# One order of steps for another: chunk attention and a multiplicative FFN on one core

## The chip, the core and the metric

The kernel runs on one core of one Trainium2 chip. The metric is the device time of one execution in microseconds (us), as the median of several runs. Engines are called as in the profile: PE (TensorE), DVE (VectorE), ACT (ScalarE), POOL (GpSimd), SP (SyncE). Each works through its own queue in order, and semaphores tie the queues together. DMAs are issued by POOL (the loads) and SP (moves and stores).

## The reference

For each of 8 batches and 8 heads, 576 tokens of width 64 are cut into chunks of 64, and attention stays within a chunk. The result, 4608 tokens of width 512, goes through a feed-forward part without a nonlinearity:

```python
scores = scale * np.matmul(q_c, k_c.transpose(0, 1, 2, 4, 3))
attn = np.exp(scores - max); attn = attn / (sum + 1e-09)
x = np.matmul(attn, v_c)              # then tokens x 512
h = (x @ w1) * (x @ w2) @ w3          # 512 -> 1024 -> 1024
out = h @ w_out                       # -> 512, float32
```

## The kernel before, in words

The work is cut into 18 **pairs** of 256 tokens (4 chunks), p = 0 to 17. The order of all instructions is written out by hand in the string ORDER (lines 9 to 40) as 606 steps; a step is a letter with numbers, and lines 447 and 448 call them one by one. Every instruction is kept behind the one before it on its own engine, so ORDER is the order of each engine's queue. Steps on different engines are tied only by data and buffers.

Steps of a pair, by engine (p is the pair, u a half of it, g = p // 2 a group of two pairs):

- POOL: `q`, `k`, `v` load a pair's queries, keys and values, and `i`, `o`, `h` the weights. `w` and `x` are one-element copies that read a result, so that the loads behind them on POOL wait for it (`x11` reads xn of pair 11).
- DVE: `T` transposes q (s = 0) or k (s = 1) of a pair within blocks of 32 into qkT. `N` takes a reciprocal and scales a half of a pair's attention output into xn. `X` transposes a half of xn, into xt for pairs 0 to 7, into xm from pair 8 on. `M` multiplies the two halves of the hidden layer into ab. `V` transposes w3.
- PE: `S` makes scores: 64 small matmuls for pairs 0 to 7, 32 from pair 8 on. `P` multiplies them with the values (64 or 32 small matmuls, into two PSUM tiles, u = 0 and 1). `A` and `B` are x @ w1 and x @ w2 for one slice j, into the two halves of one PSUM tile: 8 matmuls 256 wide for pairs 0 to 3, which have slices 0 to 3, and 4 matmuls 512 wide from pair 4 on, where slices 0 to 7 stand for two pairs at once (A4.j serves pairs 4 and 5, and so on). `W` folds w3 and w_out into w3o once. `O` makes 256 output tokens: 16 matmuls 512 wide. `D` are idle matmuls at the start.
- ACT: `E` is the exponential of a pair's scores. `C` copies A's half of the PSUM tile to SBUF, where M reads it. `Y` copies an output from PSUM to SBUF, `Z` does so for w3o. `K` converts the first q and k.
- SP: from pair 8 on, `G` moves qkT to qkm and `H` moves xm to xt by DMA between partitions (4 DMAs a step; two steps a group). `Q` stores an output.

Each PE step in code is a loop over `mm` (line 94), so all matmuls carry line 95 in the profile, and all loads line 98 and all moves line 193.

Buffers tie the queues too. **PSUM has four tiles** of two banks (line 88, `bufs=4`), shared by all of S, P (two), A with B, O and W. A tile comes free when E (of S), N (of P), M (of A and B), Y (of O) or Z (of W) has read it. In SBUF there are five qk tiles (free after T), two each of qkT, qkm, xm and e, three xn, four xt, three ab (free after both O of the group), three copies of C, two output tiles (free when stored), and six value buffers, of which pair p takes p % 6 and frees it with its P.

In short, a pair goes q, k, T, (G), S, E, P, N, X, (H), and every two pairs then A, B, C, M for eight slices, and O, Y, Q. The long steps A, B, O and W fill PE while the short ones wait for other engines.

## Time and profile before

| | |
|---|---|
| median of 3 runs | 244.46 us (244.41 to 244.48) |
| span of the profiled execution, first to last instruction | 242.9 us |
| difference of the two | 1.56 us; the profiled execution's own time is not given apart from its span |
| PE, DVE, ACT, POOL busy | 226.7, 154.3, 85.2, 83.7 us |
| matmuls and weight loads | 2753 each |
| first matmul of real work, last matmul's end | 9.8 us, 239.6 us |
| mean granted PE clock | 1.000 |
| issued from POOL and SP, by DMA queue | q0: 18.9 MB, 83.9% of 16 engines' span; q1: 17.8 MB, 24.0% |

A span is counted from the first to the last instruction of the profiled execution. "Busy" on PE is the time in which a matmul is under way; matmuls overlap. In the page's strips the span is cut into 40 slices of 6.07 us, and a digit is the busy share in tenths. In a list of waits the columns are the total in us, how often, and the longest. In an order of time the columns are start, length, engine, line, operation, tiles, count, and in brackets the idle time just before, with what ended it; "issue" stands where the profile shows nothing that was waited for. Because every engine works through ORDER in sequence and no matmul record is missing here, each record can be given to its step, and step times in this text (S7 at 86.63) come from the order of time in that way.

### The profile page before, as it was taken

The numbers are of one execution on the slowest core, as the hardware profiler recorded it, in microseconds if no ns is written. First come the engines' busy times: TensorE is split into PE (matmuls) and PEld (weight loads), VectorE is DVE, ScalarE is ACT, GpSimd is POOL, SyncE is SP. The second block draws the span as 40 slices with busy tenths as digits, with TensorE's granted clock in tenths as the row PEclk, the third lists the DMA queues.
The fourth block names the chain that finished last, engine by engine and source line by source line (L and its number), as shares of the span: only waits on it lengthen the run. The fifth ranks groups of instructions, "written<-read, shape, count | busy, mean of one in ns | idle before, by whom it ended". The sixth has DMA issues, their size and how long they took to land.

```text
span 242.9 us, 6385 instructions
## 1 busy us (share of the span) xinstructions
PE 226.7 (93%) x2753; PEld 120.2 (49%) x2753; DVE 154.3 (64%) x235; ACT 85.2 (35%) x116; POOL 83.7 (34%) x114
## 2 busy tenths in 40 slices
PE   1189989999999999999999999999999999999994
PEld 1147868874445444444444444444444444444443
DVE  1756799699799588999998899918540332143000
ACT  2412423423333344425336234162332332322322
POOL 7856976656986345764160230000000000000000
PEclk9999999999999999999999999999999999999999
DMA  6999999999999999999999793735502200400244
GB/s 173 179 185 181 185 169 200 196 193 171 167 173 218 222 228 259 179 224 196 205 236 223 221 139 91 163 88 209 142 0 89 87 0 0 173 3 1 86 173 173
DMA packets 93597, 37.65 MB, mean 155 GB/s; under 512 B 75008, under 2 KB 86528, under 8 KB 93568
## 3 DMA queue, kind: packets, MB, share of 16 engines
q0 software_dynamic: 82592, 18.88, 83.9%
q1 hardware_dynamic: 9936, 17.83, 24.0%
q10 hardware_dynamic: 1040, 0.52, 0.8%
q8 instruction: 21, 0.34, 0.6%
q14 instruction: 8, 0.07, 0.1%
HBM read 38.80 MB, written 9.44 MB: 199 GB/s over the span
## 4 chain that ended last, share of the span: by engine, by line
PE 72%; DMA 16%; DVE 4%; SPq 3%; POOL 2%; issue 1%; ACT 0%; DVEq 0%; POOLq 0%
PE ab_ps L95 39%; PE o_ps L95 23%; PE w_ps L95 6%; DMA w<-in_moe_w_dram 4%; DMA qkm<-qkT 3%; SPq L193 3%; DMA qk<-in_q_dram 3%; DMA qk<-in_k_dram 3%; DMA xt<-xm 3%; PE pv L95 2%; PE s_ps L95 2%; DVE qkT L201 2%; POOL vbuf L98 1%; POOL w L98 1%; DVE xt L297 1%
## 5 line engine op out<-in xcount | busy, mean ns | idle before, releaser
L95 PE MATMUL ab_ps<-xt,w 128*128 128x512 bf16 (+1 forms) x688 | 127.4, 342 | 0.7 <-DVE xt L297 0.6
L95 PEld LDWEIGHTS <-w 128*128 128x128 bf16 x704 | 67.1, 98 | 56.1 <-issue 1.8
L366 DVE TENSOR_TENSOR ab<-a_sb,ab_ps 128x512 bf16<-128x512 f32 x71 | 47.8, 674 | 43.4 <-ACT a_sb L351 43.1
L351 ACT COPY a_sb<-ab_ps 128x512 f32<-128x512 f32 x71 | 41.6, 586 | 81.3 <-PE ab_ps L95 81.0
L95 PE MATMUL o_ps<-w3o,ab 128*128 128x512 bf16 (+1 forms) x296 | 63.9, 373 | 0.0
L201 DVE STREAM_TRANSPOSE qkT<-qk 128x1024 bf16<-128x1024 bf16 x36 | 45.1, 1291 | 7.2 <-ACT qk L144 5.5
L95 PEld LDWEIGHTS <-ab 128*128 128x128 bf16 x296 | 28.5, 98 | 32.2
L98 POOL DMA_DIRECT2D vbuf<-in_v_dram x40 | 33.9, 855 | 20.4 <-DMA qk<-in_q_dram 5.2
L396 ACT COPY o_sb<-o_ps 128x1024 f32<-128x1024 f32 x17 | 17.2, 1012 | 45.3 <-PE o_ps L95 41.3
L264 DVE TENSOR_TENSOR xn<-pv,rcs 128x512 bf16<-128x512 f32 x36 | 24.9, 692 | 1.4
L98 POOL DMA_DIRECT2D qk<-in_q_dram x23 | 18.1, 790 | 8.9 <-DMA qk<-in_k_dram 2.4
L98 POOL DMA_DIRECT2D qk<-in_k_dram x23 | 18.0, 783 | 6.5 <-DMA vbuf<-in_v_dram 3.7
L234 ACT ACTIVATE e<-s_ps 128x1024 bf16<-128x1024 f32 x16 | 15.9, 1026 | 1.7 <-PE s_ps L95 1.3
L95 PE MATMUL w_ps<-wo,w3T 128*128 128x512 bf16 x64 | 14.0, 379 | 0.0
L305 DVE STREAM_TRANSPOSE xm<-xn 128x512 bf16<-128x512 bf16 x20 | 13.5, 696 | 0.2
L261 DVE RECIPROCAL rcs<-pv 128x8 f32<-128x8 f32 x36 | 6.9, 193 | 10.4 <-PE pv L95 10.4
L98 POOL DMA_DIRECT2D w<-in_moe_w_dram x16 | 11.1, 695 | 5.3 <-DMA wo<-in_moe_w_out_dram 2.9
L95 PEld LDWEIGHTS <-e 64*32 64x32 bf16 (+1 forms) x832 | 7.8, 97 | 8.7 <-issue 6.9
L95 PE MATMUL pv<-vbuf,e 64*32 64x65 bf16 (+1 forms) x832 | 10.2, 197 | 1.8 <-ACT e L234 1.1
L297 DVE STREAM_TRANSPOSE xt<-xn 128x512 bf16<-128x512 bf16 x16 | 11.4, 711 | 0.5
L389 DVE COPY o_sb<-o_ps 128x256 f32<-128x256 f32 x1 | 0.4, 425 | 16.0 <-PE o_ps L95 16.0
L95 PEld LDWEIGHTS <-qkT 32*64 32x64 bf16 x512 | 5.5, 117 | 10.1 <-DVE qkT L201 7.9
(29 smaller groups left out, 54.2 us busy)
## 6 DMA issues: line engine op xcount, KB each, us to landing
out_dram<-o_sb SPq DMA_DIRECT2D x17, 512.0 KB, 3.3
qkm<-qkT SPq DMA_DIRECT2D x40, 128.0 KB, 4.0
vbuf<-in_v_dram POOLq DMA_DIRECT2D x32, 128.0 KB, 8.2
w<-in_moe_w_dram POOLq DMA_DIRECT2D x16, 256.0 KB, 9.9
qk<-in_q_dram POOLq DMA_DIRECT2D x11, 256.0 KB, 6.8
qk<-in_k_dram POOLq DMA_DIRECT2D x11, 256.0 KB, 7.8
xt<-xm SPq DMA_DIRECT2D x40, 64.0 KB, 3.2
wo<-in_moe_w_out_dram POOLq DMA_DIRECT2D x4, 256.0 KB, 7.1
```

The source lines that it names most:

```text
L95: return inorder(nc.tensor.matmul(*a, **kw))
L98: return inorder(nc.gpsimd.dma_start(dst, src))
L193: inorder(nc.sync.dma_start(dst, src))
L201: inorder(nc.vector.transpose(qkT_t[g][:, :, p % 2, s, heads(h)].rearrange("p e h (y t) -> p h t e y", t=2), qk_t[p][:, s, heads(h)].rearr ...
L234: inorder(nc.scalar.activation(e_t[p][:, :, heads(hh)], s_t[p][:].rearrange("p u (h q) -> p u h q", q=CH)[:, :, heads(hh)], Exp, scale=sca ...
L261: inorder(nc.vector.reciprocal(rc, pv[:, :, :, D:W]))
L264: inorder(nc.vector.tensor_mul(xn_t[p][:, u], pv[:, :, :, 0:D], rc.to_broadcast([P, 2, 4, D])))
L297: inorder(nc.vector.transpose(new_xt(g)[:].rearrange("p (o t) -> p o t", o=KO)[:, :, t0:t0 + UT] .rearrange("p o (m y) -> p m o y", y=BL), ...
L305: inorder(nc.vector.transpose(xm_t[g][:, u, :, m].rearrange("p o (c y) -> p c o y", y=BL), xn_t[p][:].rearrange("p u r m d -> p (u r) m d" ...
L351: inorder(nc.scalar.copy(a_t[p, j][:], ps_t[p, j][:, 0, :]))
L366: inorder(nc.vector.tensor_mul(o, view(a_t.pop((p, j))[:]), view(ps_t.pop((p, j))[:, 1, :])))
L396: inorder(nc.scalar.copy(o_sb[:], ps_t.pop(p)[:]))
```

## The change

The 606 steps stay the same, none is added or left out. From the 61st on (behind B0.2) they stand in another order. Steps of one kind still take the pairs in sequence. Two lines of code are added besides: the constant 8 gets the name MOVED, and a value buffer is taken from a list of free ones at v and given back at P, in place of p % 6.

```diff
 B0.2
-C0.2 M0.1 A1.0 T2.0 B1.0 C1.0 M0.2 A1.1 T2.1 q7 k7
-v7 B1.1 C1.1 M1.0 S2 M1.1 A0.3 E2 T3.0 B0.3 C0.3 P2 M0.3 A1.2 N2.0 X2.0 B1.2 C1.2 N2.1 A1.3 X2.1
...
-C3.1 V0 A3.2 M3.1 B3.2 C3.2 V1 A3.3 M3.2 B3.3 C3.3 V2 W0 M3.3 V3 W1 Z0 V4 V5 W2 Z1 V6 V7 T5.0 Z2 W3
-T5.1 q10 k10 T6.0 T6.1 P4 v10 q11 k11 Z3 S5 N4.0 O0 E5 X4.0 N4.1 X4.1 T7.0 O1 T7.1 Y0 Q0 T8.0 P5 v11
-q12 k12 Y1 S6 T8.1 O2 Q1 E6 N5.0 X5.0 N5.1 X5.1 O3 T9.0 T9.1 Y2 G4.0 P6 v12 q13 k13 A4.0 N6.0 B4.0
-G4.1 Y3 X6.0 N6.1 C4.0 A4.1 X6.1 B4.1 C4.1 M4.0 Q2 S7 Q3 M4.1 A4.2 E7 T10.0 B4.2 C4.2 T10.1 P7 v13
-q14 k14 A4.3 M4.2 B4.3 N7.0 C4.3 A4.4 X7.0 M4.3 B4.4 C4.4 N7.1 A4.5 M4.4 B4.5 C4.5 X7.1 S8 M4.5 S9
...
-G8.1 X14.1 A10.7 M10.6 B10.7 N15.0 C10.7 O6 N15.1 M10.7 X15.0 X15.1 H7.0 S16 Y6 S17 O7 E16 E17 H7.1
-P16 Y7 O8 Q6 N16.0 Q7 N16.1 X16.0 X16.1 P17 Y8 A12.0 N17.0 Q8 B12.0 N17.1 C12.0 A12.1 X17.0 B12.1
...
+T2.0 A1.0 B1.0 M0.1 C0.2 A1.1 T2.1 B1.1 M0.2 S2
+C1.0 M1.0 C1.1 A0.3 E2 B0.3 P2 q7 M1.1 C0.3 A1.2 B1.2 M0.3 N2.0 N2.1 A1.3 C1.2 X2.0 X2.1 B1.3 A2.0
+T3.0 C1.3 B2.0 T3.1 S3 C2.0 E3 A2.1 M1.2 v7 M1.3 M2.0 A2.2 P3 B2.1 C2.1 N3.0 N3.1 X3.0 v8 X3.1 B2.2
+T4.0 M2.1 k7 q8 C2.2 A2.3 B2.3 T4.1 C2.3 A3.0 B3.0 M2.2 M2.3 C3.0 A3.1 M3.0 B3.1 S4 C3.1 V0 E4 V1
+A3.2 V2 k8 A3.3 q9 B3.2 M3.1 k9 B3.3 C3.2 W0 V3 Z0 M3.2 W1 V4 V5 V6 C3.3 Z1 W2 Z2 V7 T5.0 W3 M3.3 Z3
+T5.1 P4 S5 T6.0 N4.0 E5 N4.1 T6.1 X4.0 T7.0 T7.1 O0 v9 Y0 q10 X4.1 P5 N5.0 S6 O1 N5.1 E6 X5.0 T8.0
+Y1 P6 S7 X5.1 N6.0 T8.1 T9.0 E7 Q0 Q1 T9.1 q11 O2 k10 A4.0 Y2 N6.1 X6.0 B4.0 C4.0 G4.0 A4.1 M4.0
+C4.1 B4.1 A4.2 P7 C4.2 M4.1 B4.2 O3 X6.1 k11 T10.0 q12 N7.0 X7.0 G4.1 N7.1 A4.3 M4.2 q13 k12 T10.1
+A4.4 Y3 C4.3 B4.3 A4.5 A4.6 B4.4 C4.4 C4.5 q14 T11.0 M4.3 B4.5 S8 T11.1 M4.4 C4.6 S9 k13 X7.1 B4.6
+E8 M4.5 A4.7 B4.7 C4.7 A6.0 M4.6 E9 v10 G5.0 T12.0 G5.1 P8 C6.0 Q2 B6.0 M4.7 A6.1 N8.0 A6.2 T12.1
+N8.1 B6.1 M6.0 C6.1 q15 C6.2 B6.2 P9 M6.1 A6.3 B6.3 M6.2 X8.0 N9.0 v11 A6.4 C6.3 A6.5 N9.1 S10 C6.4
...
+E11 T13.0 B6.7 Q3 N10.1 M6.7 T13.1 O4 P11 X10.0 H4.0 H4.1 Y4 O5 k15 T14.0 A8.0 C8.0 N11.0 G6.0 N11.1
...
+k17 T16.1 B8.5 A8.6 C8.4 C8.5 A8.7 M8.4 x12 v14 B8.6 T17.0 B8.7 A10.0 B10.0 C8.6 M8.5 M8.6 C8.7 v15
+A10.1 M8.7 A10.2 C10.0 G7.1 M10.0 P13 C10.1 B10.1 B10.2 N13.0 C10.2 S14 M10.1 A10.3 N13.1 M10.2
+A10.4 B10.3 B10.4 C10.3 T17.1 E14 X12.0 C10.4 A10.5 M10.3 C10.5 P14 G8.0 M10.4 S15 N14.0 Q5 B10.5
+E15 O6 x11 v16 M10.5 P15 Y6 O7 Y7 N14.1 A10.6 X12.1 X13.0 G8.1 S16 X13.1 N15.0 S17 C10.6 Q6 E16
+B10.6 N15.1 M10.6 A10.7 X14.0 H6.0 E17 B10.7 P16 N16.0 H6.1 C10.7 A12.0 B12.0 A12.1 M10.7 C12.0
...
+B16.7 Q13 O15 M16.6 Y15 M16.7 Q14 O16 Y16 Q15 Q16 O17
...
+MOVED = 8
...
+    vb_t, vb_free = {}, list(vbuf)
...
     def load_v(p):
+        vb_t[p] = vb_free.pop(0)
...
-                load(vbuf[p % 6][at * CH:(at + m) * CH, u, :, 0:D],
+                load(vb_t[p][at * CH:(at + m) * CH, u, :, 0:D],
...
-            if p < 8:
+            if p < MOVED:
...
         e = e_t[p]
+        vb_free.append(vb_t[p])
```

By queue, the parts that the steps below speak of:

- PE before: `W3 P4 S5 O0 O1 P5 S6 O2 O3 P6 A4.0 B4.0 A4.1 B4.1 S7 A4.2`; after: `W3 P4 S5 O0 P5 S6 O1 P6 S7 O2 A4.0 B4.0 A4.1 B4.1 A4.2 P7 B4.2 O3`. PE's queue is the same in both up to `B2.0 S3 A2.1`.
- SP before: `Q0 Q1 G4 Q2 Q3 G5 H4 G6 Q4 H5 Q5 G7 H6 G8 H7 Q6 ...`; after: `Q0 Q1 G4 G5 Q2 Q3 H4 G6 H5 G7.0 Q4 G7.1 G8.0 Q5 G8.1 Q6 H6 H7 ...`.
- POOL before, from q7: `q7 k7 v7 q8 k8 v8 ...` pair by pair to v15, then `x11 q16 k16 v16 x12 q17 k17 v17`; after: `q7 v7 v8 k7 q8 k8 q9 k9 v9 q10 q11 k10 k11 q12 q13 k12 q14 k13 v10 q15 v11 q16 k14 k15 v12 k16 q17 v13 k17 x12 v14 v15 x11 v16 v17`.

More of the change, by code (lines that the diff above doesn't have):

```diff
@@ L11 @@
 v5 S0 T1.0 E0 P0 D0.1.0.4.512 T1.1 q6 k6 v6 N0.0 S1 D1.0.0.5.512 X0.0 N0.1 X0.1 A0.0 E1 B0.0 C0.0 P1
-M0.0 A0.1 N1.0 X1.0 B0.1 C0.1 N1.1 A0.2 X1.1 B0.2 C0.2 M0.1 A1.0 T2.0 B1.0 C1.0 M0.2 A1.1 T2.1 q7 k7
-v7 B1.1 C1.1 M1.0 S2 M1.1 A0.3 E2 T3.0 B0.3 C0.3 P2 M0.3 A1.2 N2.0 X2.0 B1.2 C1.2 N2.1 A1.3 X2.1
-B1.3 C1.3 M1.2 A2.0 T3.1 q8 k8 v8 B2.0 C2.0 M1.3 S3 T4.0 A2.1 E3 M2.0 B2.1 T4.1 q9 k9 C2.1 P3 v9
-M2.1 A2.2 N3.0 B2.2 C2.2 X3.0 A2.3 N3.1 B2.3 X3.1 C2.3 M2.2 S4 M2.3 A3.0 E4 B3.0 C3.0 A3.1 M3.0 B3.1
@@ L21 @@
-E8 A4.6 T11.0 B4.6 E9 T11.1 P8 v14 q15 k15 C4.6 A4.7 M4.6 G5.0 B4.7 C4.7 N8.0 A6.0 M4.7 B6.0 N8.1
-C6.0 G5.1 A6.1 X8.0 B6.1 M6.0 C6.1 X8.1 P9 v15 A6.2 M6.1 N9.0 B6.2 C6.2 N9.1 A6.3 M6.2 B6.3 C6.3
-X9.0 A6.4 M6.3 B6.4 C6.4 X9.1 A6.5 T12.0 H4.0 B6.5 C6.5 M6.4 A6.6 M6.5 B6.6 T12.1 H4.1 C6.6 S10 S11
-M6.6 E10 A6.7 T13.0 B6.7 E11 P10 T13.1 C6.7 O4 M6.7 G6.0 N10.0 N10.1 X10.0 G6.1 P11 Y4 X10.1 O5
-N11.0 N11.1 x11 q16 k16 v16 Q4 X11.0 X11.1 T14.0 A8.0 H5.0 Y5 B8.0 T14.1 C8.0 A8.1 M8.0 B8.1 H5.1
-C8.1 T15.0 A8.2 B8.2 M8.1 C8.2 T15.1 Q5 A8.3 B8.3 C8.3 M8.2 G7.0 S12 M8.3 S13 E12 A8.4 T16.0 B8.4
@@ L27 @@
-E13 G7.1 P12 T16.1 C8.4 A8.5 B8.5 M8.4 C8.5 N12.0 A8.6 M8.5 B8.6 C8.6 N12.1 x12 q17 k17 v17 A8.7
-M8.6 B8.7 C8.7 X12.0 P13 M8.7 A10.0 X12.1 B10.0 C10.0 N13.0 A10.1 M10.0 B10.1 N13.1 C10.1 A10.2
-X13.0 B10.2 M10.1 C10.2 X13.1 S14 S15 M10.2 E14 A10.3 H6.0 T17.0 B10.3 E15 P14 T17.1 C10.3 A10.4
-H6.1 M10.3 B10.4 C10.4 N14.0 A10.5 M10.4 B10.5 G8.0 C10.5 N14.1 A10.6 M10.5 B10.6 C10.6 X14.0 P15
-G8.1 X14.1 A10.7 M10.6 B10.7 N15.0 C10.7 O6 N15.1 M10.7 X15.0 X15.1 H7.0 S16 Y6 S17 O7 E16 E17 H7.1
-P16 Y7 O8 Q6 N16.0 Q7 N16.1 X16.0 X16.1 P17 Y8 A12.0 N17.0 Q8 B12.0 N17.1 C12.0 A12.1 X17.0 B12.1
@@ L33 @@
-M12.0 C12.1 X17.1 A12.2 M12.1 H8.0 B12.2 C12.2 A12.3 M12.2 B12.3 C12.3 H8.1 A12.4 M12.3 B12.4 C12.4
-A12.5 M12.4 B12.5 C12.5 A12.6 M12.5 B12.6 C12.6 A12.7 M12.6 B12.7 C12.7 O9 M12.7 O10 Y9 Q9 A14.0 Y10
-B14.0 C14.0 Q10 A14.1 M14.0 B14.1 C14.1 A14.2 M14.1 B14.2 C14.2 A14.3 M14.2 B14.3 C14.3 A14.4 M14.3
-B14.4 C14.4 A14.5 M14.4 B14.5 C14.5 A14.6 M14.5 B14.6 C14.6 A14.7 M14.6 B14.7 C14.7 O11 M14.7 O12
-Y11 Q11 A16.0 Y12 B16.0 C16.0 Q12 A16.1 M16.0 B16.1 C16.1 A16.2 M16.1 B16.2 C16.2 A16.3 M16.2 B16.3
@@ L38 @@
-C16.3 A16.4 M16.3 B16.4 C16.4 A16.5 M16.4 B16.5 C16.5 A16.6 M16.5 B16.6 C16.6 A16.7 M16.6 B16.7
-C16.7 O13 M16.7 O14 Y13 Q13 O15 Y14 Q14 O16 Y15 Q15 Y16 Q16 O17
+M0.0 A0.1 N1.0 X1.0 B0.1 C0.1 N1.1 A0.2 X1.1 B0.2 T2.0 A1.0 B1.0 M0.1 C0.2 A1.1 T2.1 B1.1 M0.2 S2
+C1.0 M1.0 C1.1 A0.3 E2 B0.3 P2 q7 M1.1 C0.3 A1.2 B1.2 M0.3 N2.0 N2.1 A1.3 C1.2 X2.0 X2.1 B1.3 A2.0
+T3.0 C1.3 B2.0 T3.1 S3 C2.0 E3 A2.1 M1.2 v7 M1.3 M2.0 A2.2 P3 B2.1 C2.1 N3.0 N3.1 X3.0 v8 X3.1 B2.2
+T4.0 M2.1 k7 q8 C2.2 A2.3 B2.3 T4.1 C2.3 A3.0 B3.0 M2.2 M2.3 C3.0 A3.1 M3.0 B3.1 S4 C3.1 V0 E4 V1
@@ new lines @@
+E8 M4.5 A4.7 B4.7 C4.7 A6.0 M4.6 E9 v10 G5.0 T12.0 G5.1 P8 C6.0 Q2 B6.0 M4.7 A6.1 N8.0 A6.2 T12.1
+N8.1 B6.1 M6.0 C6.1 q15 C6.2 B6.2 P9 M6.1 A6.3 B6.3 M6.2 X8.0 N9.0 v11 A6.4 C6.3 A6.5 N9.1 S10 C6.4
+B6.4 X8.1 B6.5 M6.3 C6.5 q16 X9.0 E10 k14 X9.1 M6.4 M6.5 A6.6 B6.6 C6.6 A6.7 C6.7 M6.6 P10 S11 N10.0
+E11 T13.0 B6.7 Q3 N10.1 M6.7 T13.1 O4 P11 X10.0 H4.0 H4.1 Y4 O5 k15 T14.0 A8.0 C8.0 N11.0 G6.0 N11.1
+A8.1 B8.0 T14.1 C8.1 B8.1 X10.1 X11.0 X11.1 A8.2 M8.0 G6.1 Y5 v12 C8.2 A8.3 M8.1 H5.0 T15.0 S12 S13
@@ new lines @@
+H5.1 k16 B8.2 T15.1 C8.3 E12 M8.2 q17 G7.0 E13 B8.3 M8.3 A8.4 Q4 T16.0 B8.4 P12 N12.0 N12.1 v13 A8.5
+k17 T16.1 B8.5 A8.6 C8.4 C8.5 A8.7 M8.4 x12 v14 B8.6 T17.0 B8.7 A10.0 B10.0 C8.6 M8.5 M8.6 C8.7 v15
[3 more added lines that the diff above has]
+B10.6 N15.1 M10.6 A10.7 X14.0 H6.0 E17 B10.7 P16 N16.0 H6.1 C10.7 A12.0 B12.0 A12.1 M10.7 C12.0
@@ new lines @@
+B12.1 M12.0 X14.1 C12.1 A12.2 M12.1 B12.2 N16.1 C12.2 X15.0 v17 A12.3 C12.3 A12.4 B12.3 A12.5 X15.1
+M12.2 M12.3 B12.4 C12.4 X16.0 C12.5 B12.5 A12.6 B12.6 M12.4 C12.6 H7.0 M12.5 M12.6 A12.7 C12.7 B12.7
+P17 H7.1 N17.0 O8 A14.0 B14.0 N17.1 M12.7 Y8 Q7 X16.1 A14.1 X17.0 O9 B14.1 H8.0 A14.2 C14.0 C14.1 Y9
+B14.2 A14.3 X17.1 M14.0 M14.1 C14.2 M14.2 Q8 H8.1 A14.4 A14.5 B14.3 B14.4 Q9 B14.5 A14.6 C14.3 C14.4
+C14.5 B14.6 M14.3 C14.6 A14.7 M14.4 C14.7 M14.5 B14.7 O10 M14.6 A16.0 Y10 B16.0 A16.1 B16.1 O11
@@ L40 @@
+C16.0 Y11 O12 M14.7 Q10 A16.2 M16.0 Y12 A16.3 B16.2 C16.1 Q11 C16.2 A16.4 C16.3 M16.1 B16.3 A16.5
+M16.2 B16.4 O13 Q12 M16.3 C16.4 B16.5 M16.4 A16.6 C16.5 O14 M16.5 Y13 B16.6 Y14 A16.7 C16.6 C16.7
+B16.7 Q13 O15 M16.6 Y15 M16.7 Q14 O16 Y16 Q15 Q16 O17
 """
+MOVED = 8
 LOW, HIGH = 2.0 ** -60, 2.0 ** 60
@@ L246, in do_P @@
             for m in range(4):
-                if p < 8:
+                if p < MOVED:
                     for g in range(NB) if hh is None else (2 * hh, 2 * hh + 1):
@@ L251, in do_P @@
                                lhsT=e[half[r], u, 2 * g + m % 2, m // 2 * BL:(m // 2 + 1) * BL],
-                               rhs=vbuf[p % 6][half[r], u, 2 * g + m % 2, 0:W], start=True, stop=True)
+                               rhs=vb_t[p][half[r], u, 2 * g + m % 2, 0:W], start=True, stop=True)
                 else:
@@ L255, in do_P @@
                         mm(pv[half[g], r, m * W:(m + 1) * W], lhsT=e[half[r], u, 4 * g + m, :],
-                           rhs=vbuf[p % 6][half[r], u, 4 * g + m, 0:W], start=True, stop=True)
+                           rhs=vb_t[p][half[r], u, 4 * g + m, 0:W], start=True, stop=True)
     def do_N(p, u):
@@ L294, in do_X @@
         g, m = divmod(p, 2)
-        if p < 8:
+        if p < MOVED:
             t0 = m * PT + u * UT
@@ L326, in do_AB @@
     def do_AB(p, j, f, which):
-        if p >= 8:
+        if p >= MOVED:
             rhs = new_xt(p // 2)[:].rearrange("p (s o t) -> p o s t", s=2, o=KO)
@@ L359, in do_M @@
             view = lambda t: t.rearrange("p (j t) -> p j t", j=2)
-        elif p < 8:
+        elif p < MOVED:
             o = ab_t[g][:, j]
```

## The prediction

> **What bounds the kernel now.** I read the busy shares first, then the waits of PE, then PE's order of time.

> ```profile
> PE 226.7 (93%) x2753; PEld 120.2 (49%) x2753; DVE 154.3 (64%) x235; ACT 85.2 (35%) x116; POOL 83.7 (34%) x114
> PEclk9999999999999999999999999999999999999999
> DMA  6999999999999999999999793735502200400244
> ```

> PE is busy for 93% at a full granted clock, and the 16 DMA engines are full until about 133 us. The waits of PE say where the rest is:

> ```profile
> PE z_ps L95 <- DVE qkT L201: 7.4, 1, 7.4
> PE z_ps L95 <- DVE zero L114: 1.4, 1, 1.4
> PE pv L95 <- ACT e L234: 1.1, 1, 1.1
> PE z_ps L95 <- issue: 1.1, 1, 1.1
> PE pv L95 <- issue: 0.7, 1, 0.7
> PE ab_ps L95 <- DVE xt L297: 0.6, 2, 0.3
> PE s_ps L95 <- issue: 0.5, 1, 0.5
> ```

> All but the last three lie before 24 us, where the order is not changed. From A1.0 (24.31) to O17 (236.01) PE takes 211.7 us. Laid end to end with the spacings of its own rows (A or B 0.874 in pairs 0 to 3 and 0.864 later, O and W 3.455, S and P 0.645 and 0.63 before pair 8 and 0.285 and 0.38 from it on, 0.10 whenever a full matmul is followed by S or P, and 0.08 after S from pair 8 on) the steps need 209.3. So an order without any wait could win 2.4 us, 1% of the time. It can lose more.

> Two waits are called "issue": PE waited for no other engine. Here they are in the order of time:

> ```profile
> 30.40 0.46 PE L95 MATMUL pv<-vbuf,e 64*32 64x65 bf16 x37
> 31.53 0.30 PE L95 MATMUL pv<-vbuf,e 64*32 64x65 bf16 x27 [0.67 <-issue]
> ...
> 86.63 0.60 PE L95 MATMUL s_ps<-qkT 32*64 32x64 bf16 x51
> 87.72 0.31 PE L95 MATMUL s_ps<-qkT 32*64 32x64 bf16 x13 [0.49 <-issue]
> ```

> Both break a step in the middle. Counted over all records of PE (weight loads, matmuls, waits), the three issue stops end at records 449 (18.51 us), 961 (31.53) and 2753 (87.72): 512 and 1792 apart, which is 2 and 7 times 256. The page has a queue that moves 16 KB pieces,

> ```profile
> q8 instruction: 21, 0.34, 0.6%
> ```

> [...]

> **The change part by part.** The v buffers: values are loaded and used in sequence, so the list gives buffer p % 6 again; nothing. MOVED is 8, as the constant was; nothing. All else is order. No instruction is added or removed.

> **Up to W0: nothing.** P2's stop stays, since PE's list up to it is the same. On DVE, M0.3, N2, X2, T3.0, T3.1 now follow each other from 31.1 us, at 0.65, 0.92, 0.71 and 1.30 less 0.08 overlap each, and T3.1 ends at 37.2; PE comes to S3 at 37.1. But block 1217 begins inside S3, and its piece (35.74) is usable near 38.1. S3 therefore ends near 38.2, as it does now (A2.1 at 38.21). From there to W0 PE does the same work in another order: W0 near 51.95, as now.

> **P4 to S7: 3.2 lost.** Now O0 and O1 stand between S5 and P5, O2 and O3 between S6 and P6. The new order is P4 S5 O0 P5 S6 O1 P6 S7 O2. The block entered at S5 (record 1985) ends after S5 (128), O0 (32) and 96 records of P5: 0.645 + 3.455 + 0.10 + 0.45 = 4.65 us. The next ends after 32 of P5, S6, O1 and 64 of P6: also 4.65. With 6.15 and 6.4 the two stops are 1.5 and 1.7. The shortest interval between two entries anywhere is 4.91, which gives 0.25 each; the slowest piece on the full engines started 5.9 after entry, which gives 3.7 each. I take the rows of the same steps.

> **Stops of now that go: 1.4 gained.** Behind W0 PE now loses 0.6 at S7, 0.28 between S10 and S11 (G5's last landing, 112.89), 0.17 at A10.0, 0.17 at A12.1, and one change from full to small matmuls less is 0.10.

> **PSUM: 1.85 lost.** There are four tiles. The new order sets several A before their B and S beside A, so that all four are in use; then the next step waits until M has read its tile. From a B's start: 1.07 to C's start, 0.585, 0.04, 0.67, 0.04 to PE, together 2.4 (B4.3 at 91.29, M4.3's end 93.66). Until that need PE does:
> - B4.4 B4.5 S8, then S9: 2 x 0.864 + 0.10 + 0.285 = 2.1; wait 0.3.
> - B4.7 A6.0 and half of P8: 2.0; wait 0.4.
> - B6.1 B6.2 P9, then A6.3: 2.2; wait 0.2. B6.6 A6.7 P10, then S11: 0.2.
> - B10.4 A10.5 P14, then S15: 2.2, but E14 (1.02) stands before C10.4 on ACT, so M10.4 ends 2.95 after B10.4's start: 0.75.

> The trace has no wait of this kind; each may be 0 (if the releases come sooner) or about 0.3 more, so 0 to 3.3 in all. I take the sums.

> **Loads.** k7 goes behind v7 and v8: 1.7 us each later, landing near 69.8; T7.1 ends at 71.2, and S7 is at 74.9 even without stops. Later q and k go ahead of v; v10 (for P10) passes nine loads, and is issued near 99, 13 us ahead of its use. On POOL x12 now holds up v14, v15, x11, v16: N12.1 ends near 133, v14 lands about 5 us later, P14 is at 147. N14.0 waits for x11 (three xn buffers), ready near 137 against 148. Without that cover each us late is a us of PE.

> **Moves on SP: 0, with thin cover.** From the last transpose to the last landing the rows give G4 11.8, G5 13.4, H4 10.8, G6 8.0, H5 about 11. The new order leaves 14.1, 15.3, 12.0, 9.1 and 12.1. Q2 and Q3 go behind G5, which helps it. Q6 now stands before H6 and waits for Y6: O6's start + 4.7, Q6 0.4, eight issues 4.4 to the last, 2 to 2.5 to land, 11.5 to 12, and A12.0 comes 12.04 after O6 plus waits. I count 0; it may be 1.

> **O's as tail.** O8 to O14 are spread among A14 and A16. M14.0 must wait for O9 and M16.0 for O11 (three ab buffers), near 184.5 and 206; the PSUM tiles wanted next, at 187 and 209, come free by then. The last steps O15, O16, O17 and their copies and stores have the distances of now. Nothing.

> **Sum.** +3.2 - 1.4 + 1.85 = +3.65. PE's last matmul moves from 239.64 to 243.3, the span from 242.9 to 246.5. The runs' median 244.46 is 1.56 above the span of the profiled execution; I leave that as it is: **248.1 us**, 1.5% slower.

> **Rivals.**
> 1. Not slower: the block supply doesn't limit, the stops at P2 and S7 being accidents of their places. For it: only three of some 20 entries show a stop. Against it: the multiples of 256, and the pieces before each. It decides at 4.65 us from entry to the usable block. P5 and P6 then run through (-3.2), P2's 0.67 goes and S3 waits for T3.1 instead (0.9 with X2.1): -0.4 against now at W0. 244.46 - 0.4 - 1.4 + 1.85 = 244.5. With PSUM waits shorter than my sums it is faster, down to 242.7 with none.
> 2. Transfers come late: loads that x11 and x12 now hold back run beside G6, H4, H5, each with about 1 us of cover, and Q6 holds H6. Some 3 more: 251. For it: landings of 6 to 9 us where the engines are full. Against it: the extra waits of PE give the moves time.
> 3. PSUM tiles are bound to the release that stands last in the order of steps, not to the one that comes first in time. Then A2.1 waits for E3 (1.2), O7 for Y6 (0.8), A10.6 for Y7 (1.25), O12 for Y11 (1.25), by 4.7 from an O's start to its Y's end (O9 to Y9) against 3.46 of O: 4.5 more, 252.6.

> **How the numbers follow.** The forecast has 0.66, rival 1 0.15 (0.05 of it faster, 0.07 the same), rival 2 0.12, rival 3 0.05; 0.02 is left for an order whose waits nearly all vanish (0.01 faster, 0.01 same). About 0.2% (0.5 us) is what a measurement of this kernel can tell from no change. Small block waits (0.5 in place of 3.2) with PSUM as summed give 245.4; block waits of 2.5 each and rival 2 in part give 251.3. Some of the forecast's low side falls within 0.2%: 0.03. Faster 0.06, same 0.11, slower 0.83; range 245.2 to 251.3.

> **What will show it.** Right: issue stops of 1 to 2 us inside P5 and P6, at records 256 apart; no stop at S7; W0 near 52; waits of PE for DVE ab at S9, A6.3, S11 and S15 of 0.2 to 0.8; last matmul near 243. Wrong: P5 and P6 unbroken (rival 1), waits for DMA at S12, A8.0, A10.0 or A12.0 (rival 2), or for ACT after O6, O7 and O11 (rival 3).

## The result, and the profile after

| | before | after |
|---|---|---|
| median, us | 244.44 (244.24 to 244.48, 4 runs) | 255.75 (255.62 to 258.34, 4 runs) |
| span of the profiled execution, us | 242.9 | 253.4 |
| A1.0 starts, W0 starts, us | 24.31, 51.95 | 24.05, 51.27 |
| PE's last matmul ends, us | 239.64 | 250.16 |

The change makes the kernel slower: after over before is 1.049 by the means of the runs, with an interval of 1.0445 to 1.0535 (1.046 by the medians). The forecast was 248.1 with a range to 251.3, so the direction was right and the size was not. The line numbers of the new kernel are 1 higher at `mm` (L96), 5 at M (L371) and C (L356).

The page of the new kernel, busy shares and strips:

```profile
PE 229.3 (90%) x2753; PEld 120.4 (48%) x2753; DVE 153.0 (60%) x235; ACT 83.8 (33%) x116; POOL 83.6 (33%) x114
PEclk9999999999999999999999999999999999999999
DMA  7999999999999999999574997420504302220424
```

PE does the same 2753 matmuls at a full clock, and its share falls from 93% to 90%: PE stands still more. The waits of PE in the new kernel (what waited, for what, us in total, times, longest):

```profile
PE ab_ps L96 <- ACT a_sb L356: 6.8, 9, 1.2
PE pv L96 <- issue: 1.9, 2, 1.7
...
PE s_ps L96 <- DVE ab L371: 0.9, 2, 0.7
PE s_ps L96 <- DVE qkT L205: 0.5, 1, 0.5
PE ab_ps L96 <- DMA xt<-xm: 0.4, 1, 0.4
...
PE pv L96 <- DVE ab L371: 0.3, 1, 0.3
```

The last five were forecast in kind: stops inside P, S waiting for M's release of a PSUM tile, S3 waiting for T3.1, A12.0 for H6, and P8 for M's release of a tile. The first line is the largest, and nothing in the prediction speaks of it: PE waits for ACT's C. Before, this pair does not occur in the list.

Idle time in this list is shorter by some 0.17 us than what a wait costs (for B4.1 0.67 and 0.84), because a full matmul's record is 0.38 us long where the next one starts 0.216 after it (0.864 for the four of a slice). So I counted as the prediction did, from start to start, against the spacings of PE's own rows. From A1.0 to O17 the excess is 2.4 us before and 13.15 after. In the new kernel, the places above 0.06, by cause:

| cause | steps | us |
|---|---|---|
| B starts only when its own C has ended | B4.1 B4.2 B4.3 B4.5 B6.0 B6.2 B10.6 B12.5 B12.7 B14.7 B16.3 B16.7 | 9.03 |
| blocks of 256 PE instructions | P5 0.32, P6 1.70, P2 0.13 | 2.15 |
| S waits for a PSUM tile | S11 0.22, S15 0.77 | 0.99 |
| transposes and moves | S3 0.52, A2.0 0.10, A12.0 0.43 | 1.05 |

At B6.0, P8's wait for a tile (0.3 in the list) lies under the 0.90 that is put down to C.

The block stops, in PE's order of time in the new kernel (start, length, engine, line, operation, count, idle time before):

```profile
70.00 0.58 PE L96 MATMUL pv<-vbuf,e 64*32 64x65 bf16 x51
70.77 0.24 PE L96 MATMUL pv<-vbuf,e 64*32 64x65 bf16 x13 [0.20 <-issue]
...
75.14 0.43 PE L96 MATMUL pv<-vbuf,e 64*32 64x65 bf16 x34
77.23 0.31 PE L96 MATMUL pv<-vbuf,e 64*32 64x65 bf16 x30 [1.66 <-issue]
```

P5 breaks after 51 matmuls and P6 after 34. The two stops end at records 2242 and 2498, 256 apart, and the 16 KB pieces at 68.35 and 74.78 start 2.4 us before each end (2.3 to 2.6 in the kernel before). S7 is now whole.

The new kind of wait, first on PE (the end of B4.0 and A4.1, then B4.1 and A4.2):

```profile
82.68 1.68 PE L96 MATMUL ab_ps<-xt,w 128*128 128x512 bf16 x7
85.02 1.89 PE L96 MATMUL ab_ps<-xt,w 128*128 128x512 bf16 x8 [0.67 <-ACT a_sb L356]
```

and on ACT in the same stretch (C4.0, C4.1):

```profile
83.52 0.58 ACT L356 COPY a_sb<-ab_ps 128x512 f32<-128x512 f32 x1 [0.67 <-PE ab_ps L96]
84.39 0.58 ACT L356 COPY a_sb<-ab_ps 128x512 f32<-128x512 f32 x1 [0.28 <-PE ab_ps L96]
```

C4.1 ends at 84.39 + 0.58 = 84.97, and B4.1 starts 0.05 later, though B4.1 reads nothing of C4.1: C4.1 reads A's half of the tile, B4.1 writes the other half. The new order has `A4.1 M4.0 C4.1 B4.1`: C stands **ahead of the B of its own slice**. In ORDER before, C stands behind its B at every slice. In the new one 22 C's stand ahead (C4.1 C4.2 C4.3 C4.5 C4.6, C6.0 C6.2 C6.4 C6.7, C8.0 to C8.3, C10.1 C10.5 C10.6, C12.3 C12.5 C12.7, C14.7, C16.3 C16.7). For each of the 22, B starts after C's end, and for 12 of them PE loses time by it.

The trace of the kernel before shows the same tie from the other side. C reads A's half alone, but in all 72 slices it starts only when B has ended, within 0.06 us. For C12.2 on ACT:

```profile
172.32 0.59 ACT L351 COPY a_sb<-ab_ps 128x512 f32<-128x512 f32 x1 [1.14 <-PE ab_ps L95]
```

A12.2 had ended at 171.42, B12.2 ended at 172.28.

The price depends on what PE has to do between A and B. With nothing, A's last matmul ends 1.03 after A's start, and C takes 0.58, with a step of 0.04 and one of 0.05 on either side: B starts 1.70 after A where 0.86 would do, 0.84 lost (B4.1, B12.7, B14.7, B16.7). Where C must also wait on ACT behind another C, it is 1.3. ACT around B12.5 in the new kernel (the two copies C12.4 and C12.5 in one line), and PE there:

```profile
178.94 1.07 ACT L356 COPY a_sb<-ab_ps 128x512 f32<-128x512 f32 x2 [2.87 <-PE ab_ps L96]
```

```profile
175.71 3.19 PE L96 MATMUL ab_ps<-xt,w 128*128 128x512 bf16 x14
180.06 3.61 PE L96 MATMUL ab_ps<-xt,w 128*128 128x512 bf16 x16 [1.16 <-ACT a_sb L356]
```

C12.4 waits for B12.4 (its end 178.90), C12.5 goes behind it and ends at 180.01, and B12.5 starts at 180.06.

### The profile page after: what moved, and what is told of

It reads as the page before. It is cut to its first block, busy times and chain, and to the rows that moved or that the text cites. A ratio compares the mean times of both kernels' runs of the same rounds, so it can differ in the third digit from the quotient of the medians.

```text
span 253.4 us, 6402 instructions
## 1 busy us (share of the span) xinstructions
PE 229.3 (90%) x2753; PEld 120.4 (48%) x2753; DVE 153.0 (60%) x235; ACT 83.8 (33%) x116; POOL 83.6 (33%) x114
## 4 chain that ended last, share of the span: by engine, by line
PE 80%; DVE 6%; ACT 5%; issue 3%; DMA 3%; SPq 2%; DVEq 0%
PE ab_ps L96 43%; PE o_ps L96 23%; PE w_ps L96 5%; ACT a_sb L356 4%; PE z_ps L96 3%; PE s_ps L96 3%; PE pv L96 2%; DMA raw<-in_q_dram 2%; DVE qkT L205 2%; SPq L197 2%; DVE xn L269 2%; DVE ab L371 1%; DVE xt L302 1%; DMA xt<-xm 1%; ACT e L238 1%
## 5 line engine op out<-in xcount | busy, mean ns | idle before, releaser
L96 PE MATMUL ab_ps<-xt,w 128*128 128x512 bf16 (+1 forms) x688 | 129.5, 342 | 7.7 <-ACT a_sb L356 6.8
L96 PEld LDWEIGHTS <-w 128*128 128x128 bf16 x704 | 67.3, 98 | 63.7 <-issue 9.8
L371 DVE TENSOR_TENSOR ab<-a_sb,ab_ps 128x512 bf16<-128x512 f32 x71 | 47.7, 678 | 67.2 <-ACT a_sb L356 36.8
L356 ACT COPY a_sb<-ab_ps 128x512 f32<-128x512 f32 x71 | 41.0, 587 | 85.9 <-PE ab_ps L96 85.9
L96 PE MATMUL o_ps<-w3o,ab 128*128 128x512 bf16 (+1 forms) x296 | 64.7, 374 | 0.0
L205 DVE STREAM_TRANSPOSE qkT<-qk 128x1024 bf16<-128x1024 bf16 x36 | 45.7, 1291 | 5.5 <-ACT qk L145 5.3
L96 PEld LDWEIGHTS <-ab 128*128 128x128 bf16 x296 | 28.4, 98 | 32.3
L96 PE MATMUL w_ps<-wo,w3T 128*128 128x512 bf16 x64 | 14.0, 380 | 0.0
L96 PE MATMUL pv<-vbuf,e 64*32 64x65 bf16 (+1 forms) x832 | 10.5, 198 | 3.3 <-issue 1.9
L96 PEld LDWEIGHTS <-e 64*32 64x32 bf16 (+1 forms) x832 | 7.9, 97 | 10.5 <-issue 7.9
L412 DVE STREAM_TRANSPOSE w3T<-w 128x1024 bf16<-128x1024 bf16 x8 | 9.3, 1216 | 1.7 <-DMA w<-in_moe_w_dram 1.7
## 6 DMA issues: line engine op xcount, KB each, us to landing
w<-in_moe_w_dram POOLq DMA_DIRECT2D x16, 256.0 KB, 9.8
qk<-in_q_dram POOLq DMA_DIRECT2D x11, 256.0 KB, 10.6
qk<-in_k_dram POOLq DMA_DIRECT2D x11, 256.0 KB, 10.6
wo<-in_moe_w_out_dram POOLq DMA_DIRECT2D x4, 256.0 KB, 7.1
```

The costliest lines, as they stand in the source:

```text
L96: return inorder(nc.tensor.matmul(*a, **kw))
L205: inorder(nc.vector.transpose(qkT_t[g][:, :, p % 2, s, heads(h)].rearrange("p e h (y t) -> p h t e y", t=2), qk_t[p][:, s, heads(h)].rearr ...
L356: inorder(nc.scalar.copy(a_t[p, j][:], ps_t[p, j][:, 0, :]))
L371: inorder(nc.vector.tensor_mul(o, view(a_t.pop((p, j))[:]), view(ps_t.pop((p, j))[:, 1, :])))
L412: inorder(nc.vector.transpose(w3T_t[f][:].rearrange("p k (f y) -> p f k y", y=BL), w3[:, NB * f:NB * (f + 1), :].rearrange("p f (k x) -> p ...
```

## The experiments

The theory after the result: **a C ahead of its B makes B wait for C** and costs 9.0 us; the rest is blocks, tiles and one move. The rival readings: PE and ACT get in each other's way on one PSUM tile, or PE is late for another reason, and C's end stands before B's start by accident. Runs made together share runs of the kernel before; their medians were 244.57 (e1 to e4), 244.68 (e5 to e8) and 244.77 us (e9 to e11). The traces of e5 to e11 lack 22 of PE's 2753 matmul records each, so step times from them are good to some 0.2 us.

### e2: the suspected cost alone, put into the kernel before

C12.0 to C12.7 go ahead of their B; nothing else.

```diff
-... Y8 A12.0 N17.0 Q8 B12.0 N17.1 C12.0 A12.1 X17.0 B12.1 M12.0 C12.1 X17.1 A12.2 M12.1 H8.0 B12.2 C12.2 ...
+... Y8 A12.0 N17.0 Q8 C12.0 B12.0 N17.1 A12.1 X17.0 C12.1 B12.1 M12.0 X17.1 A12.2 M12.1 H8.0 C12.2 B12.2 ...
```

> The kernel before, with the eight copies C12.0 to C12.7 put right ahead of their B instead of behind it. Theory 1: each B12.j starts 1.70 us after its A (1.03 for A, 0.04, 0.59 for C, 0.04) in place of 0.86, so eight times 0.84 = 6.7 us more: 251.1. Rival (PE stops in the changed kernel for want of PSUM tiles): M frees its tile no later than now, so nothing, 244.4, or a little faster, as C is done sooner.

Measured: 251.62 us (250.93 to 252.12), ratio 1.0285 (1.0251 to 1.032). PE in a stretch of pair 12; each line is B12.j with the next A:

```profile
171.58 1.89 PE L95 MATMUL ab_ps<-xt,w 128*128 128x512 bf16 x8 [0.67 <-ACT a_sb L351]
174.14 1.89 PE L95 MATMUL ab_ps<-xt,w 128*128 128x512 bf16 x8 [0.67 <-ACT a_sb L351]
```

In the kernel before, the same matmuls run without a break:

```profile
171.69 8.58 PE L95 MATMUL ab_ps<-xt,w 128*128 128x512 bf16 x39
```

Now a slice takes 2.56 us in place of 1.73. Seven B's lose 0.84 each, and B12.0 loses 1.41, as C12.0 waits behind Y8: 7.3 in all, measured 7.05. Eight exchanged steps on ACT's queue cost 2.9% of the kernel.

### e9: the same order, but B writes a tile of its own

For pair 12, B takes another PSUM tile than A.

```diff
-                mm(ps_t[p, j][:, which, i * n:(i + 1) * n],
+                mm((ps_t, pb_t)[which][p, j][:, which, i * n:(i + 1) * n],
...
+        pb_t[p, j] = psum("b_ps") if p == 12 else ps_t[p, j]
```

> The kernel before with C12.0 to C12.7 ahead of their B, as in the kernel that took 251.6 us, but B12.0 to B12.7 write a PSUM tile of their own in place of the second half of A's tile. Theory 1a (B waits for C because both use one tile, and the wait is kept per tile, not per half): the eight stops of 0.84 go, and four tiles are enough for A12.j, B12.j and the next pair: 244.5 us, between 244 and 245.3. Rival 1b (PE can't write PSUM at full pace while ACT reads it, or C ahead costs by its place on ACT): the stops stay, 250 or more.

Measured: 245.64 us (244.9 to 245.99), ratio 1.0031 (1.0016 to 1.0047). PE in the same stretch:

```profile
171.72 1.03 PE L95 MATMUL ab_ps<-xt,w 128*128 128x512 bf16 x4
172.58 1.03 PE L95 MATMUL b_ps<-xt,w 128*128 128x512 bf16 x4
173.45 1.03 PE L95 MATMUL ab_ps<-xt,w 128*128 128x512 bf16 x4
```

The steps follow each other by 0.86 again, with C still ahead of B. So PE keeps its 0.86 here while ACT reads another tile, and C's place does no harm by itself. In this program the wait is kept **for the whole tile**: in the new kernel's 22 slices and the eight of e2, B stands behind C and starts after C's end though it writes the other half, and in the 72 slices of the kernel before, C stands behind B and starts after B's end though it reads the other half. The written order decides which waits for which. What is left above the kernel before, 0.9 us (244 to 245.3 was expected), has its place: B12.0's own tile is one that O8 used, and B12.0 waits 1.2 us for Y8 to read it.

### e1: the new kernel with each C right behind its B

```diff
-C4.1 B4.1 A4.2 P7 C4.2 M4.1 B4.2 ... A4.4 Y3 C4.3 B4.3
+B4.1 C4.1 A4.2 P7 M4.1 B4.2 C4.2 ... A4.4 Y3 B4.3 C4.3
...
-C16.6 C16.7 B16.7
+C16.6 B16.7 C16.7
```

> The changed order, but each of the 22 copies C that stand ahead of their own B are put right behind it; all else stays. Theory 1 (B may not write its half of a PSUM tile until a C that stands ahead of it has read the other half; the changed kernel loses 9.0 us of PE at 12 such B's): those stops vanish. Some of the tile waits that the prediction summed come back (S9 0.3, P8 0.4, A6.3 0.2), since PE is no longer late there. 255.7 - 9.0 + 0.9 = 247.6 us, between 246.5 and 249. Rival (PE stops there because all four PSUM tiles are in use and ACT is late; where C stands doesn't matter): above 253.

Measured: 250.7 us (250.17 to 252.84), ratio 1.0268 (1.0221 to 1.0316). That is above the 246.5 to 249 expected. All twelve stops are gone, but only 5 of the 9 us come back. PE's waits in e1:

```profile
PE pv L96 <- issue: 2.4, 3, 1.6
...
PE s_ps L96 <- DVE ab L371: 1.0, 3, 0.7
PE ab_ps L96 <- DVE ab L371: 0.8, 3, 0.5
```

No line for a_sb is left, and waits for M's release of a tile (DVE ab) are more. Start to start the excess is 8.5: 2.0 for P5 and P6, 0.65 at P2, and 2.05 for the tile waits at S9, P8, A6.3, S11 and S15, three of which were covered in the new kernel because PE came late there anyway. Another 1.36 are tile waits at A8.4, A8.5, A8.6 and A10.3: C8.2 and others now come later, and with them M and the release. A12.0 loses 0.59. The last 1.6 us are of a kind that I hadn't expected. The windows of e1 around the stop in P6 (window, us, then per engine busy time and count for PE, PEld, DVE, ACT and POOL, then granted PE clock, DMA share, GB/s):

```profile
76.00:78.00 2.00, 0.56 (x67) 0.52 (x69) 1.97 (x4) 0.49 (x1) 0.49 (x1) 1.00 1.58 260
78.00:80.00 2.00, 2.00 (x52) 0.92 (x41) 2.00 (x3) 1.02 (x1) 0.81 (x2) 0.55 1.91 177
80.00:82.00 2.00, 2.00 (x7) 0.77 (x6) 1.97 (x4) 0.00 (x0) 1.03 (x2) 0.59 1.42 287
```

After the 1.64 us stop (77.44) the granted clock is about half for 3 us, and O2 takes 1.58 longer. The two runs with a mean clock of 1.000 took 250.17 and 250.51, so the kernel's time hangs on this by less than 1.58; what takes the place of the dip in them was not profiled.

### e3 and e4: shift the block limits in the kernel before

PE's first step makes 12 or 40 more idle matmuls (their results are read by nobody), and every later block limit falls 24 or 80 records earlier in the work.

```diff
-R0 R1 v0 q1 k1 i0 v1 i1 i2 q2 k2 v2 i3 q3 k3 v3 q4 k4 v4 o h0 h1 D0.0.0.16.64 K0 T0.0 K1 T0.1 q5 k5
+R0 R1 v0 q1 k1 i0 v1 i1 i2 q2 k2 v2 i3 q3 k3 v3 q4 k4 v4 o h0 h1 D0.0.0.28.64 K0 T0.0 K1 T0.1 q5 k5
```

(e4: `D0.0.0.56.64`.)

> The kernel before, with 12 more idle matmuls (24 records of PE) in its first step, where PE has nothing to do until 9.8 us. Theory 2 (PE's instructions come in blocks of 256, usable some 5.0 to 5.3 us after PE enters the block ahead): all later block limits move 24 records forward in the order. The one in P2 falls early in P2 and leaves a stop of 0 to 0.15, the one in S7 falls where no stop is left: 0.8 to 1.4 us faster, 243.1 to 243.7. Rival (the stops in P2 and S7 are accidents of those steps): no change, 244.4, the stops in the same matmuls as now.

> The kernel before, with 40 more idle matmuls (80 records of PE) in its first step, again within the time in which PE waits for the first transposes. Theory 2: the limits move 80 records forward and fall so that two of them are crossed quickly three times: stops near 40 us (2.4), 75 us (3.0) and 90 us (1.7) in place of 1.2 in all, at records 193 more than a multiple of 256: some 5 us slower, 248 to 250. Rival (accidents of P2 and S7, or the idle matmuls' own time): 244.4 to 244.6.

e3: 245.66 us (244.52 to 246.9, 12 runs), ratio 1.0043 (1.0022 to 1.0063). Expected was a gain, so the time was a miss. The mechanism is seen: S7's stop moves from its 51st matmul to its 39th and halves (0.49 to 0.25 idle), and the one in P2 is gone. But the gain isn't kept: in this profile A1.0 comes 0.33 later, A2.0 waits 0.71 for X2.1 in place of 0.45, and 0.29, 0.28 and 0.64 appear at S4, P6 and S17. That these follow from the stops that went is not shown: A2.0's wait is 0.5 to 1.1 in e2, e7, e9, e10 and e11 too, where the order up to there is that of before.

e4: 254.09 us (253.69 to 254.54), ratio 1.0391 (1.0358 to 1.0424), slower as expected and by more. PE around S6 in e4:

```profile
79.64 0.67 PE L95 MATMUL s_ps<-qkT 32*64 32x64 bf16 x59
84.01 0.23 PE L95 MATMUL s_ps<-qkT 32*64 32x64 bf16 x5 [3.70 <-issue]
```

This stop of 3.70 us, and another of 2.50 in P3 (43.96), end at records 2497 and 1474, within one record of 4 times 256 apart, and the pieces at 81.60 and 41.77 start 2.4 and 2.2 us before their ends. After each the granted clock is half (0.50 from 86 to 88 us and from 44 to 46), which costs another 1.7 and 1.4 us. A1.0 comes 1.4 later: behind a stop of 1.0 us, now inside S1, the five idle matmuls take 2.31 us in place of 1.25. The 40 matmuls themselves cost nothing, since the wait for the first transposes shrinks by as much (5.18 us in place of 7.36) and S0 starts at 9.78, as before (9.82). Forty idle matmuls in the first microseconds cost 9.5 us, by the places at which PE's instruction blocks begin and by the slow stretches behind the stops. That the supply of blocks can set the end is shown with this: at the stops of these runs, the next block was usable 4.3 to 7.1 us after PE's entry into the one before.

### e5: e1 with the old PE order from O1 to A4.2

```diff
-O0 P5 S6 O1 P6 S7 O2 A4.0 B4.0 A4.1 B4.1 A4.2 P7 B4.2 O3
+O0 O1 P5 S6 O2 O3 P6 A4.0 B4.0 A4.1 B4.1 S7 A4.2 P7 B4.2
```

(PE's part; Y and E move with it on ACT.)

> The changed order with each C behind its B (250.7 us), and PE's 14 steps from O1 to B4.2 put back as they were in the kernel before (O0 O1 P5 S6 O2 O3 P6 A4.0 B4.0 A4.1 B4.1 S7 A4.2), with their Y and E on ACT. Theory 2 (blocks of 256 of PE's instructions; stops of 0.33 in P5 and 1.68 in P6 in the kernel it starts from): these two go, and a stop of about 0.5 in S7 is back: 1.5 less, 249.2, between 248.4 and 249.7. Rival (P6 stops for want of something in that stretch that the place of O doesn't change, such as e or values): no change, 250.2 to 251.

Measured: 253.6 us (253.33 to 253.98), ratio 1.0358 (1.0315 to 1.0401). A miss: 2.9 us slower than e1, not faster. The stops in P5 and P6 are gone, S7's is back (0.5), and A4.0 starts at 82.61 (83.44 in e1, with the half clock ahead of it), but P6 now comes at 81.97 in place of 75.37. N6 needs P6 and stands ahead of T8.1 and T9 on DVE's queue in the new order, so the transposes (from 83.32, in e1 from 77.15), G4 behind them and the scores of pairs 8 and 9 come late. PE in e5 there:

```profile
98.06 0.21 PE L96 MATMUL s_ps<-qkm 64*64 64x64 bf16 x1 [0.49 <-DMA qkm<-qkT]
100.39 1.12 PE L96 MATMUL s_ps<-qkm 64*64 64x64 bf16 x63 [2.12 <-DMA qkm<-qkT]
```

and then the clock is half again (0.50 from 102 to 104 us). So the new order of O and P isn't free to be undone: DVE's order is built on it. What the two block stops cost by themselves is not measured by this run.

### e6 and e8: S and P later where they waited for a tile

e6 is e1 with S8 and S9 behind B4.6, P8 behind B6.0, S15 behind B10.5, and Q6 behind H6.1. e8 is e5 with the same moves.

```diff
-B4.5 C4.5 S8 T11.1 M4.4 S9 k13 X7.1 B4.6 ... P8 Q2 B6.0 ... S15 N14.0 Q5 B10.5
+B4.5 C4.5 T11.1 M4.4 k13 X7.1 B4.6 S8 S9 ... Q2 B6.0 P8 ... N14.0 Q5 B10.5 S15
```

> The changed order with each C behind its B (250.7 us), and four places mended: S8 and S9 behind B4.6, P8 behind B6.0, S15 behind B10.5 (each gives M one more slice of time to free its PSUM tile), and Q6 behind H6.1. Theory 3 (waits for a PSUM tile, as summed in the prediction, and the store in front of H6): S9 0.32, P8 0.53, S15 0.76 and A12.0 0.59 go: 2.2 less, 248.5, between 248 and 249.2. Rival (what is spared is lost again at the next tile, since M is late for it too): above 249.8.

> The changed order with each C behind its B, and the edits of both other kernels of this kind: PE's steps from O1 to B4.2 back as before, and the four places mended. If the terms simply add: 250.7 - 1.5 - 2.2 = 247.0, 1.0% above the kernel before; what is left is A8.4 with A8.6 and A10.3 (1.3), A6.3 and S11 (0.4) and S3. Rival (the terms cover each other): 248 or more.

e6: 250.04 us (248.66 to 251.92), ratio 1.0227 (1.0164 to 1.0291). The waits at S9, P8 and S15 are gone (1.6 in e1), and A12.0's falls from 0.59 to 0.15. About 1.0 us comes back as waits of 0.29 to 0.35 at A4.7, A6.2 and O6. The interval overlaps that of e1, so the two medians decide nothing between them. e8: 252.26 us (249.88 to 252.74), ratio 1.0279 (1.0217 to 1.034), with a single wait of 1.8 us at S9 for G4 and the half clock behind it. Both took longer than expected (248.5 and 247.0). Each undone edit moves the loss, or part of it, to a neighbour.

### e7, e10 and e11: can S7's stop be won in the kernel before?

In e10, S7 and E7 go behind B4.2, P7 behind B4.3, and Q2, Q3 behind G5. e11 is the move of Q2 and Q3 alone. e7 is e10 with one load in a wrong place: v13, which overwrites the value buffer of pair 7, stands ahead of P7, so pair 7 is computed with pair 13's values.

```diff
-M4.0 Q2 S7 Q3 M4.1 A4.2 E7 T10.0 B4.2 C4.2 T10.1 P7 v13 q14 k14 A4.3 M4.2 B4.3
+M4.0 M4.1 A4.2 T10.0 B4.2 S7 C4.2 E7 T10.1 A4.3 M4.2 B4.3 P7 v13 q14 k14
```

> The kernel before, with S7 (and E7) behind A4.2 and B4.2, P7 behind B4.3, and the stores Q2 and Q3 behind G5. Theory 2 says that S7's stop (0.58) goes, since PE enters that block 1.7 us later; Q2 and Q3 no longer run beside G5, so S11's wait for G5 (0.28) may go too: 243.6 to 243.9. Rival (what is won is given back at the next wait that is as yet hidden, as with the 12 idle matmuls): 244.4 or more.

> The kernel before, with S7 (and E7) behind B4.2, P7 behind B4.3 and the loads v13, q14, k14 still behind P7, and the stores Q2 and Q3 behind G5. Theory 2: S7's stop for a block of instructions (0.58) goes, as PE enters the block 1.7 us later, and G5's last landing no longer holds S11 (0.28): 0.86 less, 243.6 to 243.9. Rival (what is won is given back at the next hidden wait): 244.4 or more.

> The kernel before, with the stores Q2 and Q3 behind G5 on SP and nothing else. Theory: G5's landing, which holds S11 for 0.28, comes sooner by what the two stores took of the DMA engines: 0.2 to 0.3 less, 244.2 to 244.4. Rival: G5 is issued when T11 is done and Q2 and Q3 have landed by then (their landings are at 95.8 and 97.5, G5's first issue at 99.5), so nothing, or the stores now delay G5's own landings and H4: 244.5 to 245.

e7: 257.91 us, ratio 1.0544 (1.0507 to 1.0581). P7 has to wait 12.4 us for v13's transfer; the run says nothing on S7. e10: 244.75 us (244.45 to 245.65, 12 runs), ratio 1.000 (0.9986 to 1.0015); expected was a gain of 0.86. S7 is whole, and the time is given back right behind it. PE in e10 (A4.4 behind P7):

```profile
92.69 2.53 PE L95 MATMUL ab_ps<-xt,w 128*128 128x512 bf16 x10 [0.71 <-DVE ab L366]
```

P7 now holds two of the four tiles, and A4.4 has to wait for the one that M4.2 reads; M4.2 stands behind T10.0 and T10.1 on DVE (89.59 to 92.08) and ends at 92.64. e11: 244.46 us (244.19 to 245.2, 12 runs), ratio 0.9988 (0.9974 to 1.0002). S11's wait for G5 (0.28) is gone in its profile, and the median is 0.3 lower, as expected; but the interval takes in no change, so this measurement can't tell.

## Why the prediction was wrong, point by point

**Up to W0: 0 forecast, 0.7 gained.** P2's stop should have stayed; in the new kernel's profile it is 0.13 in place of 0.73, because its piece started 2.1 us after PE entered the block before, not 2.5. S3's block, which the prediction had at 38.1, was there before PE came to it at 37.34. In e1, with the same PE order up to there, P2's stop is 0.65. So this term moves by half a us from one execution to the next. Over all profiles W0 starts at 51.3 to 52.0 with the new order up to there, and at 51.8 to 52.4 with the old one. S3 waits 0.52 for T3.1, which the prediction named under its first rival.

**P4 to S7: 3.2 forecast, 2.0 measured.** Place and kind were right: stops inside P5 and P6, at records 256 apart, none at S7. The intervals between block entries were right as well (4.65 forecast; 4.62 and 4.76 without the stops). The size of one failed: the block behind S5's entry was usable after 4.94 us, where 6.15 was taken from the kernel before. For P6 6.46 was measured and 6.4 forecast. The reading that a block is asked for about when PE enters the one before goes by the starts of the 16 KB pieces alone (their distances are in the last section). Rival 1 is out.

**Stops of now that go: 1.4.** Right: S7, S10 to S11, A10.0 and A12.1 show none. The five numbers there add to 1.32; S7's stop costs 0.68 from start to start, not 0.6, which makes it 1.4.

**PSUM: 1.85 forecast.** Right in mechanism and size, but covered in part. In e1, without the waits for C, the five places show 0.32, 0.53, 0.22, 0.22 and 0.76, together 2.05, where 0.3, 0.4, 0.2, 0.2 and 0.75 were summed. In the new kernel itself only S11 and S15 lose by it (0.99): PE reaches S9 and A6.3 late, and P8's wait lies under that of B6.0 for C6.0.

**Loads and O's tail: 0.** Right: no wait of PE for a load or for Y shows between A1.0 and O17.

**Moves on SP: 0, or 1 for Q6 ahead of H6.** A12.0 waits 0.43 for H6. Rival 2 would have needed 3.

**The step that failed** is "All else is order": it put the place of C against B at nothing, without a reason. The PSUM sums even start C 1.07 us after B's start, that is, behind B everywhere, and the new order has it ahead at 22 slices. Rival 3 asked whether waits are bound to the written order, but for the release of a tile to another step, where they are not (A2.1, O7, A10.6 and O12, the places that it named, follow without a wait). Within one tile they are: at all 22 slices with C ahead, B starts 0.05 us or more after C's end. The term is +9.03, by e2 0.84 for each exchanged pair, and by e9 nothing when the two halves are two tiles.

The sum, made again with what was measured: 3.65 forecast; blocks -1.2, tiles -0.85, A12.0 +0.4, before W0 -0.7, C ahead of B +9.0. That gives +10.3, against 10.5 between the two spans. (The medians are 11.3 apart; the profiled execution has the shortest span of the four, 253.4 against 254.1, 254.3 and 256.0.) Without C ahead of B the same sum leaves +1.3, so the forecast had the direction for a sound reason, but most of the loss has another cause. The prediction could have found it: the front of this text says that A and B go into two halves of one tile and that C reads A's, the diff shows `A4.1 M4.0 C4.1 B4.1`, and in the trace before each C waits for B's half, which it doesn't read.

What stays open: what the block stops cost by themselves in the new order (e5 changed DVE's waits with it), and the exact worth of the half clock in e1. No run has ACT reading one half of a tile while PE writes the other, since the wait keeps them apart. No version here is faster than the kernel before by more than the measurement can tell.

## What to carry to other kernels

When the order of a queue written by hand is changed, list for each buffer the reads and writes in the new order, and look for a write that has come behind a read which it does not need; its price was the read's whole way there and back (0.84 us each time with nothing else between), and a tile of its own took it away (e9). An order is a set of covers: of the edits here that took stops away, e1 gave back nearly half of them at other places, e6 about half by its profile, and e3, e5, e8 and e10 kept nothing of it in their times, so price the place behind a stop before you price the stop. Where an engine stops for no reason in the profile, count its records and look for equal distances (256 here).

## What was not expected of the hardware

**The granted clock after a stop.** In these runs 3.41 us at half clock follow stops of 1.6 us (e1, e6), 1.8 (e8), 2.12 (e5), 2.50 and 3.70 (e4), and cost 1.4 to 1.7 us where it was counted (e1, e4, e6). In e7 the half clock lasts through the rest of the 12.4 us stop and 3.8 us more. But the new kernel's stop in P6 of 1.66 us, at the same place as e1's, is followed by 1.00.

The traces show more. Counted from a trace's first record of a full clock, every change of the granted clock in all 13 traces falls on a whole multiple of 3.41 us (in the kernel before the full clock is recorded for 228.69 us, 67 times 3.413, in the new one for 235.52, 69 times), and not on the stops themselves: in e1 the stop ends at 77.44 and the half clock begins at 78.21. In e1 the stretch of 3.41 us with the stop and the next one, and in the new kernel the one with the stop (columns as above):

```profile
74.80:78.21 3.41, 1.77 (x129) 1.15 (x129) 3.38 (x5) 1.01 (x1) 1.20 (x2) 1.00 1.71 247
78.21:81.62 3.41, 3.41 (x33) 1.31 (x20) 3.38 (x6) 1.02 (x1) 1.64 (x3) 0.50 1.68 222
```

```profile
75.60:79.01 3.41, 1.78 (x99) 1.23 (x100) 3.38 (x6) 1.34 (x2) 0.30 (x1) 1.00 1.70 232
```

PE is busy alike in both stretches with the stop (1.77 and 1.78), but with O's full matmuls (128 rows and columns of PE) for 0.64 us in e1 and 0.88 in the new kernel. Before PE's last matmul the clock falls seven times in these traces, and the stretch ahead of each fall has full matmuls for 0.15 to 0.85 us; apart from the stretches inside e7's long stop, which stay at half, the new kernel's is the only other one there under 1.2. The time of all matmuls doesn't tell them apart: e6's stretch ahead of its fall was busy for 1.85 us, small matmuls of S and P included, more than the new kernel's 1.78. So two stops of the same length at the same place, 1.64 and 1.66 us, came with half clock in one execution and without it in the other, and what was found to differ is where the stretches lie and how long full matmuls ran in them. No run was made to test whether that decides it. One of the new kernel's four runs (258.34 us) has a mean clock of 0.993, as the profiled runs of e1 and e6 with their one half stretch have.

**Blocks of instructions.** From PE's entry into a block to the usable next one it took 4.3 to 7.1 us at the stops of these runs (4.34 at P2 and 6.46 at P6 of the new kernel, 7.11 at S7 in e3), of which the last 2.2 to 2.6 us pass after the 16 KB piece starts. In the kernel before and in the new one, 21 such pieces and 21 entries follow each other one by one: up to 130 us a piece starts 0.6 to 5.9 us behind its entry, later from 4.5 us ahead of it to 1.8 behind. S and P of pairs 0 to 7 have 128 records in 0.65 and 0.63 us, and in the new order PE came to a limit 4.62 and 4.76 us after the one before, the stops not counted.
